# The value projection of three chunks by seven products for eight, and an emission clock that counts PSUM banks

## The chip, the cores and the metric

The kernel runs on one core of a Trainium2 chip. The metric is the time of the program on the device in microseconds (us); the profile adds, for one execution, every instruction's start and duration on each engine: TensorE (PE; its weight loads are listed as PEld), VectorE (DVE), ScalarE (ACT), GpSimd (POOL) and SyncE (SP, which here only issues DMAs).

## What is computed

Two layers, each an attention block A and a feed-forward block B, with the same weights in both. S = 2048 rows, D = 1024, F = 3584, everything in bf16 at the interface.

```python
def _A_ref(x, wqkv, wo):
    H = 32; Dh = D // H
    W, dil = 8, 2
    qkv = (x @ wqkv).reshape(B, S, 3, H, Dh) ...   # q, k, v
    idx = pos[:, None] - off[None, :]              # each row sees 8 rows: itself, -2, ..., -14
    logits = jnp.einsum("bhsd,bhswd->bhsw", q, kg) * scale
    attn = _softmax(jnp.where(mask, logits, -1e9), axis=-1)
    o = jnp.einsum("bhsw,bhswd->bhsd", attn, vg)
    return o... @ wo

def _B_ref(x, w1, w3, w2):
    return (silu(x @ w1) * (x @ w3)) @ w2

x = x + _A_ref(_layernorm(x), A_wqkv, A_wo)
x = x + _B_ref(_layernorm(x), B_w1, B_w3, B_w2)
# and both once more
```

## The kernel before

**Tiling.** The rows are cut in four chunks of 512 (`CH`); a pair (layer, chunk) is a unit, units 0 to 7. The normalised rows of a unit are written transposed (features on the partitions) into `xnT`, of which two buffers exist. q, k and v of a chunk are computed by `q_part`: for each of eight blocks of 128 output features, eight matmuls of 128x512 accumulate in one PSUM bank (L836), ScalarE copies the bank to SBUF (L840), and each pair of blocks is stored to DRAM (`qkv_d`, L847). Attention reads it back in halves of 256 rows: VectorE multiplies and adds in trees (`score_steps` from L576, `value_steps` from L647), TensorE gathers the heads (L604), VectorE takes the maximum and subtracts it (L625, L628), ScalarE takes the Exp (L629), and GpSimd's queue broadcasts the result (L644). The output projection is `o_tile` (L771).

**Order of the units.** q, k and v of all chunks of layer 0 come first, then the B stages of units 0 to 7 (`b_stage`). After the B stages of units 1, 2, 3 and 4 stand q, k and v of units 4, 5, 6 and 7, that is of layer 1's chunks.

**Seven products for eight.** The B stages of units 2 to 7 use Winograd's form of the two-by-two block product (`products`, `pipeline`): the features and the rows are split in halves, and seven products P1 to P7 of half size take the place of eight. For each group of 512 output features one product is eight matmuls of 128x256 (L1052). The block sums of the weights are made once, during units 0 and 1: ScalarE scales a block to FP16 (L910), VectorE forms four sums and differences (`differences`, L922), and GpSimd's queue stores them in DRAM (`t_d`). They come back as an "early" tile of 1 MB (for P1, P5, P6, P2) and a "late" tile of 768 KB (for P7, P3, P4). The sums of `xnT` are made by VectorE in `norm_sums` (L298), in three buffers that all units share; the fourth is made in place in `xnT`, once nothing needs the plain rows. In `pipeline`, a group's P1, P5, P6, P2 alternate with the group before's P7, P3, P4:

```python
for i in range(n + 1):
    for name, tail in (("P1", "P7"), ("P5", "P3"), ("P6", "P4"), ("P2", None)):
```

PSUM banks A, B and D of a group are linked by copies: P1 is copied from A to B (L1064) before P6 may add to A; P5 is kept aside (L1069); A is copied after P6 (L1073) and added to D (L1076) before P3; after P7, VectorE combines A with the kept P5 into the corner (L1088 or L1090), which P4 waits for. In the B stages the last group's tail is filled with the first products of w2 (L1165).

**What sets the order.** No scheduler reorders the instructions: each engine's queue holds them as the Python code emits them. The code carries its own clocks while it emits: `now["pe"]`, `now["dve"]`, `now["act"]` and those of the DMA. `pe`, `dve`, `act` and `dma` advance them by fixed costs. `background(until)` lets VectorE's queued work (sums, normalisations, trees) in where by these clocks it ends before the given time; `act_background` does so for ScalarE up to `gate`, 2.2 us beyond TensorE's clock; `pe_requests` emits a gather of heads once its input is 3.5 us old. `between` lets weight loads, output projections and normalisations in. Weights come through six buffers in the order of the list `seq`; `release(n)` frees buffers and so lets the next n loads go to SP's queue. Six PSUM banks serve the matmuls (`psum`), two the gathers and the output projection (`side`).

Of the kernel before, what the change touches and what calls it, by code (L numbers as in the profile page):

```python
# [17 lines left out]
def kernel(  # L18
# [137 lines left out]
    opened = [0]  # L156

    def side_tile(*args, **kw):

        while opened[0]:  # L160
            assert head(makes) is not None
            take(makes)
        return side.tile(*args, **kw)

    def bank(name):
        if name == "po":
            return side_tile([P, 512], FP32, name=name, tag="sd")
        return psum.tile([P, 512], FP32, name=name, tag="mm")
# [48 lines left out]
    size2 = const.tile([P, 16], FP32, name="size2")  # L217
    total = const.tile([P, 1], FP32, name="total")
# [4 lines left out]
    h16 = hT[:].bitcast(FP16)  # L223
    t2_d = [dram.tile([P, 7, (b - a) // 2, 512], FP16, name=f"t2_d{i}") for i, (a, b) in enumerate(fsplits)]
    t_d = [[dram.tile([P, 14, KT // 2, P], FP16, name=f"t_d{m}_{g}") for g in range(NG)] for m in range(2)]
    qkv_d = [[dram.tile([P, KT, S], BF16, name=f"qkv_d{l}_{i}") for i in range(3)] for l in range(2)]
# [74 lines left out]
    adds, acts, makes, reads, parts, sizes = [], [], [], [], [], []  # L301
# [61 lines left out]
    def act_background():  # L363
        for queue in (acts, sizes, parts, reads):
# [211 lines left out]
    def score_steps():  # L576

        V = nc.vector
        for g, (l, h) in enumerate(halves):
# [20 lines left out]
            def gather_heads(t, parts_=parts_):  # L600
                at["L"] = L = side_tile([P, W, BLK], FP32, name="L", tag="sd")
                for i in range(parts_):
# [24 lines left out]
            def exps():  # L627
                V.tensor_tensor(L[:], L[:], mx[:].unsqueeze(1).to_broadcast([P, W, BLK]), op=ALU.subtract)  # L628
                nc.scalar.activation(E[:], L[:], ACTF.Exp, scale=scale)  # L629
                at["E"] = act(0.65, now["dve"] + 0.1, "exp")  # L630

# [47 lines left out]
    for u in range(len(units)):  # L679
# [14 lines left out]
        if 1 <= u and u + 3 < len(units):  # L694
            seq += [("qkv", which, h) for which in range(3) for h in range(2)]
    w_tiles, w_at, due, used = [], {}, [], [0]

    def load_weight(pieces=1):
# [25 lines left out]
        else:  # L724
# [4 lines left out]
            if rest[0]:  # L729
                got = {}  # L730
                parts.append([weight_size(*rest[0], w, at, got), None])
                reads.append([weight_sums(*rest[0], w, got), None])
# [22 lines left out]
    def o_tile():  # L755
# [12 lines left out]
        for hh in range(2):  # L768
            ps = bank("po")
            for t in range(KT):  # L770
# [6 lines left out]
            dve(0.64, r)  # L777
# [6 lines left out]
    def queue_q(q):  # L784
# [4 lines left out]
        
# [30 lines left out]
    def q_part(l, c, which, ws, then=()):  # L820
# [8 lines left out]
        for t0 in range(0, KT, SG):  # L829
            i = (c * 3 + which) * KT // SG + t0 // SG  # L830
            i = i % (7 if l == 0 else 8) * SG
            sgt = big[:, i * CH:(i + SG) * CH].bitcast(BF16).rearrange("p (a t) -> p a t", a=SG) if l == 0 else hT[:, i:i + SG, :]
            for t in range(t0, t0 + SG):
                ps = bank("ps")
                for kk in range(KT):
# [6 lines left out]
                if first:  # L842
                    nc.scalar.copy(kT[:, t, HALO:], ps[:, 0:TCH])
                    done = act(0.3)
                if t < t0 + SG - 1:
                    pe_requests(2)
            nc.sync.dma_start(qkv_d[l][which][:, t0:t0 + SG, c * CH:(c + 1) * CH], sgt)  # L847
            landed = dma(256, done)
            if l == 0:
                stored[:] = landed, landed  # L850
# [6 lines left out]
        if which == 1:  # L857
            plain_left.discard(("Q", l, c))
        if which == 2:
# [56 lines left out]
    pending, stored, made, held = [0] * 2, [0.0] * 2, set(), []  # L916
    junk = hsum[:].bitcast(BF16).rearrange("p k t -> p (k t)")

    def differences(m, g, a, r):

        b = blocks[a]
# [3 lines left out]
        pending[a] -= 1  # L925
# [487 lines left out]
```

## Time and profile before

| what | value |
|---|---|
| median of 3 runs (lowest, highest) | 1532.38 us (1532.05, 1533.98) |
| the profiled execution | 1532.70 us |
| its span, first to last instruction | 1531.0 us |
| q, k, v of units 4 to 7 (L836), starts at | 514, 701, 885 and 1073 us |
| B stages by seven products, first matmul at | 556 us |
| VectorE's tree products, 128x2048 (L590, L665) | 1.22 us each |
| VectorE's sums of 1024 FP16 elements (L298) | 0.69 us each |
| ScalarE's copy of a bank (L840, L1064) | 0.585, 0.575 us |
| early tile, issue to landing | 6.9 us (median) |

A page of the profile has the busy time of each engine, the span in 40 slices, the DMA queues, the chain of work that ended last (followed back from the last instruction, each step to what released it), the costliest groups of instructions (line, engine, operation, output<-input, shapes, count, busy us, mean ns of one, idle time before them and what ended it) and the DMA issues. Besides the page, single views can be asked for: the chain in order of time (start, duration, what), the waits (who waited for whom, total us, times, longest) and the timeline of a stretch (start, duration, instruction, in brackets the idle time before it and what ended it). Matmuls overlap, so that the mean of one is its latency and not what it adds to the run.

### The profile page before, as it was taken

The page shows a single profiled execution, that of the slowest core. Times are in us where ns is not written, and L with a number is a line of the kernel's source. Part 1 is how long each engine was busy: PE and PEld are TensorE (multiplying, and loading weights), DVE is VectorE, ACT ScalarE, POOL GpSimd, SP SyncE. Part 2 cuts the span into 40 slices and gives each one's busy share as a digit, 9 for nine tenths or more (in the row PEclk, how much of TensorE's full clock was granted, in tenths as well). Part 3 has the DMA queues.
Part 4 walks back from the last instruction along what each step waited for, and adds up shares of the span by engine and source line. Part 5 has one row for each costly group of instructions (what it writes and reads, how often), then busy time and mean ns, then how long its engine had stood idle before and what let it go on. Part 6 is the DMA issues. An engine that isn't in the chain of part 4 may idle for free.

```text
span 1531.0 us, 25095 instructions
## 1 busy us (share of the span) xinstructions
PE 1518.1 (99%) x9594; PEld 989.5 (65%) x9634; DVE 1201.8 (78%) x2126; ACT 884.1 (58%) x1388; POOL 153.7 (10%) x308
## 2 busy tenths in 40 slices
PE   9999999999999999999999999999999999999999
PEld 7666644444444577575786767766677767686865
DVE  4688998889989898989698958898678986435445
ACT  3885476567665357455565564756557445554643
POOL 1210102121211101001011010100111000000000
PEclk9999999999999999999999999999999999999999
DMA  9777969798997888979779997898969988878885
GB/s 321 202 218 215 253 226 330 272 304 289 306 320 247 280 316 294 347 264 303 263 269 324 346 268 282 280 323 302 323 225 333 338 296 282 306 272 334 318 294 203
DMA packets 261432, 439.56 MB, mean 287 GB/s; under 512 B 73856, under 2 KB 201088, under 8 KB 245056
## 3 DMA queue, kind: packets, MB, share of 16 engines
q1 hardware_dynamic: 248464, 390.90, 76.8%
q0 software_dynamic: 12704, 46.93, 8.6%
q8 instruction: 75, 1.23, 0.3%
q14 instruction: 45, 0.37, 0.1%
q10 hardware_dynamic: 144, 0.13, 0.0%
HBM read 345.90 MB, written 67.90 MB: 270 GB/s over the span
## 4 chain that ended last, share of the span: by engine, by line
PE 97%; ACT 1%; issue 1%; DVE 0%; DMA 0%; SPq 0%; ACTq 0%
PE st L1052 32%; PE ps L836 21%; PE w L1165 16%; PE po L771 7%; PE pg L1279 6%; PE pu L1288 6%; PE acc L1310 6%; PE pq L444 1%; PE L L604 0%; DMA wqkv<-in_A_wqkv_dram 0%; ACT L629 0%; ACT L1227 0%; ACT E L629 0%; ACT sg L1227 0%; DVE x_sb L1150 0%
## 5 line engine op out<-in xcount | busy, mean ns | idle before, releaser
L836 PE MATMUL ps<-xnT,wqkv 128*128 128x512 f16 (+1 forms) x1469 | 320.4, 379 | 0.2
L1052 PEld LDWEIGHTS <-early 128*128 128x128 f16 x2688 | 262.6, 98 | 40.4 <-issue 3.5
L836 PEld LDWEIGHTS <-wqkv 128*128 128x128 bf16 x1472 | 210.6, 144 | 108.1 <-issue 2.2
L1165 PE MATMUL w<-t,hT 128*128 128x512 f16 x1008 | 226.0, 379 | 0.6 <-ACT big L1185 0.5
L1052 PEld LDWEIGHTS <-late 128*128 128x128 f16 x2016 | 197.2, 98 | 30.6 <-issue 2.5
L590 DVE TENSOR_TENSOR tree<-qT,kT 128x2048 bf16<-128x2048 bf16 x128 | 156.3, 1221 | 35.8 <-DMA kT<-qkv_d 18.2
L1052 PE MATMUL st<-xnT,late 128*128 128x256 f16 x1344 | 174.2, 273 | 2.2 <-ACT big L1073 2.2
L510 DVE TENSOR_TENSOR tree<-tree 128x1024 bf16<-128x1024 bf16 x256 | 175.6, 686 | 0.9
L1052 PE MATMUL st<-big,early 128*128 128x256 f16 x1344 | 172.3, 273 | 1.6 <-ACT sg L1227 1.1
L1165 PEld LDWEIGHTS <-hT 128*128 128x128 f16 x1008 | 98.2, 98 | 112.9 <-DVE hT L1136 2.0
L1052 PE MATMUL st<-xnT,early 128*128 128x256 f16 x1344 | 165.7, 273 | 0.0
L665 DVE TENSOR_TENSOR tree<-At,vT 128x2048 bf16<-128x2048 bf16 x128 | 156.2, 1221 | 11.9 <-DMA At<-E 10.7
L1064 ACT COPY st<-st 128x512 f32<-128x512 f32 x84 | 48.3, 575 | 128.1 <-PE st L1052 127.4
L771 PE MATMUL po<-wo,oT 128*128 128x512 bf16 x486 | 110.8, 379 | 1.3
L840 ACT CAST hT<-ps 128x512 bf16<-128x512 f32 x96 | 55.8, 585 | 90.6 <-PE ps L836 88.3
L1288 PE MATMUL pu<-xnT,w3t 128*128 128x512 f16 x448 | 105.8, 379 | 0.0
L1279 PE MATMUL pg<-xnT,w1t 128*128 128x512 f16 x448 | 105.8, 379 | 0.0
L1310 PE MATMUL acc<-w2t,hT 128*128 128x512 bf16 x437 | 97.8, 379 | 0.6
L1076 DVE TENSOR_TENSOR st<-st,big 128x512 f32<-128x512 f32 x84 | 58.4, 695 | 46.9 <-ACT big L1073 46.8
L1227 ACT ACTIVATE sg<-st,down_scale 128x512 bf16<-128x512 f32 x126 | 86.6, 687 | 11.6 <-PE st L1052 11.0
L1052 PE MATMUL st<-big,late 128*128 128x256 f16 x672 | 87.1, 273 | 0.0
L771 PEld LDWEIGHTS <-oT 128*128 128x128 bf16 x512 | 50.1, 98 | 55.7
(167 smaller groups left out, 1916.6 us busy)
## 6 DMA issues: line engine op xcount, KB each, us to landing
early<-t_d SPq DMA_DIRECT2D x84, 1024.0 KB, 6.9
late<-t_d SPq DMA_DIRECT2D x84, 768.0 KB, 6.2
t<-t_d SPq DMA_DIRECT2D x42, 1024.0 KB, 7.3
t<-t_d SPq DMA_DIRECT2D x42, 768.0 KB, 5.3
wqkv<-in_A_wqkv_dram SPq DMA_DIRECT2D x28, 1024.0 KB, 8.1
w1t<-in_B_w_dram SPq DMA_DIRECT2D x14, 1024.0 KB, 7.6
w3t<-in_B_w_dram SPq DMA_DIRECT2D x14, 1024.0 KB, 11.0
t_d<-big POOLq DMA_DIRECT2D x28, 512.0 KB, 6.2
```

Of the source, the lines that this page charges most:

```text
L510: nc.vector.tensor_tensor(b, b, buf[:, 4:8, :], op=ALU.add)
L590: V.tensor_tensor(pr, qT[:], kT[:, :, k0:k0 + TCH], op=ALU.mult)
L665: V.tensor_tensor(tm.rearrange("p w (a e) -> p w a e", a=4), At[:].rearrange("p a w e -> p w a e"), win, op=ALU.mult)
L771: nc.tensor.matmul(ps[:], lhsT=oT[:, t, j * P:(j + 1) * P], rhs=wo[:, t, hh * 512:(hh + 1) * 512], start=(t == 0), stop=(t == KT - 1))
L836: nc.tensor.matmul(ps[:], lhsT=ws[kk // KH][:, kk % KH, t::KT], rhs=xnT[:, kk, :], start=(kk == 0), stop=(kk == KT - 1))
L1052: nc.tensor.matmul(out[:, a, :], lhsT=w[:, a, blk, k, :], rhs=rhs[:, k, :], start=start and a == 0 and k == 0, stop=k == KQ - 1, skip_grou ...
L1076: nc.vector.tensor_tensor(G["D"][:], G["D"][:], su, op=ALU.add)
L1165: nc.tensor.matmul(out[:], lhsT=lhs[:, k, j * P:(j + 1) * P], rhs=w[:, k, :], start=start and k == 0, stop=k == nq - 1, skip_group_check=True)
L1227: nc.scalar.activation(sg[:], src, ACTF.Silu, scale=inv)
L1279: nc.tensor.matmul(pg[:], lhsT=w1t[:, kk, fi * P:(fi + 1) * P], rhs=xnT[:, kk, :], start=(kk == 0), stop=(kk == KT - 1))
L1288: nc.tensor.matmul(pu[:], lhsT=w3t[:, kk, fi * P:(fi + 1) * P], rhs=xnT[:, kk, :], start=(kk == 0), stop=(kk == KT - 1))
L1310: nc.tensor.matmul(acc[:], lhsT=hT[:, f, j * P:(j + 1) * P], rhs=tiles[hh][f // nq][:, f % nq, :], start=(f == 0), stop=(f == f1 - f0 - 1))
```

## The change

v of units 5, 6 and 7 (layer 1's chunks 1 to 3) is computed by seven products: two groups of 512 output features, in `pipeline`, by the new function `v_products`. The block sums of v's weights are made once, in unit 4's stage after the B stage of unit 1. There v is now computed first, then q, then k, and v's two weight buffers are held until the sums are made. The scale of the weights needs the sum of their squares, which ScalarE takes in eight passes of 1024 elements in a new queue of lowest priority (`lazy`) while layer 0's q, k and v are computed. In the stages of units 5 to 7, q and k stay plain, and the sums of `xnT` are also made for v.

The second part is in the clocks: `turn` and `free` keep, for each of the two PSUM pools, the time at which each bank's last reader is done, and a new tile pushes `now["pe"]` to the time of the bank that it takes. Every place that takes a bank records it. `finish_sums` lets other VectorE work in before the step that it forces, and w2's scalings are put ahead of queued weight scalings that nothing waits for yet.

The diff, cut to its core (the recording of banks is shown once for each kind):

```diff
+    rings = dict(mm=[], sd=[])
+    def turn(tag, bufs):
+        ring = rings[tag]
+        if len(ring) >= bufs:
+            now["pe"] = max(now["pe"], ring[-bufs])
+        ring.append(0.0)
+        return ring, len(ring) - 1
+    def free(at, t):
+        ring, i = at
+        ring[i] = t + 0.1
+    def mm_tile(shape, name):
+        turns["mm"] = turn("mm", 6)
+        return psum.tile(shape, FP32, name=name, tag="mm")
...
+    size_v = const.tile([P, 8], FP32, name="size_v")
+    blocks += [hT[:, 9:16, :].bitcast(FP16).rearrange("p b (k c) -> p b k c", k=KT // 2)]
+    t_d += [[dram.tile([P, 14, KT // 2, P], FP16, name=f"t_dv_{g}") for g in range(2)]]
...
-        for queue in (acts, sizes, parts, reads):
+        for queue in (acts, sizes, parts, reads, lazy):
...
-            seq += [("qkv", which, h) for which in range(3) for h in range(2)]
+            seq += [("qkv", which, h) for which in ((2, 0, 1) if u == 1 else (0, 1)) for h in range(2)]
+            if u > 1:
+                seq += [("early", 2, 0), ("early", 2, 1), ("late", 2, 0), ("late", 2, 1)]
...
             ps = bank("po")
+            slot = turns["sd"]
...
-            dve(0.64, r)
+            free(slot, dve(0.64, r))
...
+        if q > NCH:
+            adds.append([sum_later(key), None])
...
+    def size_of_v(i, w, at):
+        for k in range(KH):
+            yield 1.10, at, lambda: nc.scalar.activation(junk[:, 0:D], w[:, k], ACTF.Square,
+                                                         accum_out=size_v[:, KH * i + k:KH * i + k + 1])
+        if i == 1:
+            total_scale(size_v, up_v, down_v, got_v)
+    def sums_of_v(ws, at):
+        while "at" not in got_v:
+            yield "blocked"
+        stored[2] = at
+        for g in range(2):
+            for a in range(2):
+                while pending[1] and pending[2]:
+                    yield "blocked"
+                slot = min((i for i in (1, 2) if not pending[i]), key=lambda i: stored[i])
+                pending[slot] += 1
+                b = blocks[slot]
+                for i, (kh, fh) in ((0, (0, 0)), (1, (0, 1)), (3, (1, 0)), (5, (1, 1))):
+                    t = 4 * g + 2 * fh + a
+                    yield 0.65, max(at, got_v["at"], stored[slot]), lambda: nc.scalar.activation(
+                        b[:, i], ws[kh][:, :, t::KT], ACTF.Copy, scale=up_v[:])
+                makes.append([differences(2, g, a, now["act"] + 0.1, slot), None])
+        made.add("v")
...
+    def v_products(l, c):
+        key = ("Q", l, c)
...
+        def consume(G, q, src, r):
+            pair, t0 = q % 2, HT * (q // 2)
+            to = stage(G, pair)
+            if q != 3:
+                nc.scalar.activation(to[:, :, t0:t0 + HT], src, ACTF.Copy, scale=down_v[:])
+                r = act(0.57, r)
+            end = r
+            G["left", pair] -= 1
+            G["at", pair] = max(r, G.get(("at", pair), 0.0))
+            if not G["left", pair]:
+                t = 4 * G["g"] + 2 * pair
+                nc.sync.dma_start(qkv_d[l][2][:, t:t + SG, c * CH:(c + 1) * CH], to)
...
+        pipeline(key, groups, consume, lambda i: between(False, i == 0), True)
+        xnT_free[key] = now["pe"]
...
+            if (c, which) == (1, 0):
+                for i in range(2):
+                    lazy.append([size_of_v(i, w_tiles[4 + i], 40.0), None])
...
-            for which in range(3):
-                if which == 2:
-                    between(False, True)
-                q_part(*units[q], which, [weight("qkv"), weight("qkv")])
+            if u == 1:
+                for which in (2, 0, 1):
+                    if which == 1:
+                        between(False, True)
+                    ws = [weight("qkv"), weight("qkv")]
+                    if which == 2:
+                        ready = max(w_at[used[0] - 1], now["pe"])
+                        reads.append([sums_of_v(ws, ready), None])
+                    q_part(*units[q], which, ws, (), 1, 4)
+                    if which == 2:
+                        continue
+                    if which == 0:
+                        finish_sums(lambda: "v" in made)
+                        release(2)
+                    release(2)
+                force(makes, lambda: not any(pending))
+                continue
+            for which in range(2):
+                q_part(*units[q], which, [weight("qkv"), weight("qkv")], (), 1)
                 release(2)
+            v_products(*units[q])
```

In the changed file the lines move: the matmuls of `pipeline` stand at L1118 there, its copies at L1132 (P1), L1138 (P5) and L1142 (P6), the Exp at L656 and the plain projections at L869.

## The prediction

> **What bounds the kernel now.** I read the page's busy table and chain first, to see which engine sets the end; then the groups by line, for what one matmul costs; then the list of waits on TensorE, for what is left besides matmuls; then the timeline around the longest of these waits.
>
> ```profile
> span 1531.0 us, 25095 instructions
> ...
> PE 1518.1 (99%) x9594; PEld 989.5 (65%) x9634; DVE 1201.8 (78%) x2126; ACT 884.1 (58%) x1388; POOL 153.7 (10%) x308
> ...
> PE 97%; ACT 1%; issue 1%; DVE 0%; DMA 0%; SPq 0%; ACTq 0%
> ```
>
> TensorE is the bound: 97% of the chain is PE. A busy PE need not be at its peak, so I take the cost of a matmul from the chain in order of time, where uninterrupted runs stand:
>
> ```profile
> 830.14 34.93 PE st L1052 x320
> ...
> 895.83 31.23 PE ps L836 x144
> ```
>
> A product of 256 columns ("st", the seven-product form) costs 34.93/320 = 0.1092 us, one of 512 columns ("ps", plain q, k, v) 31.23/144 = 0.2169 us there, with a small gap inside; the neighbouring run of 48 gives 10.36/48 = 0.2158, which I use. The means of 379 and 273 ns in the groups are latencies of overlapping matmuls and are not added up.
>
> ```profile
> PE st L1052 <- ACT big L1073: 2.2, 1, 2.2
> ...
> PE st L1052 <- ACT sg L1227: 1.1, 1, 1.1
> PE w L1165 <- ACT big L1185: 0.5, 1, 0.5
> PE st L1052 <- ACT st L1064: 0.4, 1, 0.4
> ```
>
> What is left besides matmuls in layer 1: single waits for ScalarE. From the starts of successive matmuls they are 1.25 us (at 668), 2.36 (987), 0.63 (1065), 0.28 (1159) and 0.57 (1233), together 5.1 us; the view shows less because ends are modelled. Layer 0 has no wait above 0.22 us after 10 us. The longest one, in the timeline:
>
> ```profile
> 983.33 0.69 DVE L628 TENSOR_TENSOR L<-L,mx 128x512 f32<-128x512 f32 x1
> ...
> 984.19 1.28 ACT L629 ACT_TABLE_LOAD   x1
> 985.48 0.60 ACT L629 ACTIVATE E<-L 128x512 bf16<-128x512 f32 x1
> 986.10 1.28 ACT L1227 ACT_TABLE_LOAD   x1
> ...
> 989.16 0.58 ACT L1073 COPY big<-st 128x512 f32<-128x512 f32 x1
> ...
> 989.79 1.03 PE L1052 MATMUL st<-xnT,late 128*128 128x256 f16 x8 [2.19 <-ACT big L1073]
> ```
>
> The softmax's Exp stands in ScalarE's queue ahead of four copies that TensorE needs. Between the start of its table load and the end of the copy at L1073 lie 5.55 us. All five waits are of this kind: they depend on where the emission puts one Exp.
>
> [...]
>
> **The change, part by part.** (Starts and orders are from the instruction order of the changed kernel; durations from the trace of before.)
>
> *Matmuls.* Three chunks lose 64 products of 512 columns each, 192 x 0.2158 = 41.4 us, and gain 2 groups x 7 x 8 of 256 columns each, 336 x 0.1092 = 36.7 us. All lie on TensorE, which is the path: **-4.7 us**. The one size matmul in layer 0 costs about 0.1 (0.11 us behind each such matmul in the trace).
>
> *Work on the other engines, beside the matmuls.* ScalarE loses 24 copies (0.585) and gains 8 squares of 1024 (about 1.1, as L318), 16 scalings (0.71, as L910) and 36 evacuations (about 0.62): +27 us of 647 idle. VectorE gains 16 differences (0.42), 12 sums (0.69) and 12 combinations (0.7): +23 us of 329 idle. The squares are in layer 0, where each copy has six banks (6 x 1.73 us) of room. The scalings need 11 us of ScalarE in v and q of u=1, which last 28 us and hold 9 us of copies. I take zero for both; if that cover is gone, a late block delays only loads needed 14 us later. Two loads of 1 MB give way per chunk to four, 3.5 MB in all; they are issued before or in the k part, 14 to 28 us ahead, against 7 us to landing: zero, up to 2 us in all. The stores of t_dv go past POOL's queue ahead of At, which waits for VectorE there anyway (310.8 us in the waits): zero. On SP the v stores wait for ScalarE as before.
>
> *The end of each v pass.* Unlike the feed-forward's, its last P3 is followed by P4 with no w2 product between. P4 needs the corner that VectorE makes from P7: 0.2 us to start, 0.75 (L1088), 0.05 to release, against 0.87 of P3 as cover: 0.13 us at least. VectorE is in order, and ahead of the corner stand queued trees. Counting from the k part's end (it releases the in-place P7 sum, which heads the queue), with operations that overlap a little (0.62 for 1024 elements, 1.15 for 2048), the first chunk's corner ends at 11.9 to 12.5 us, P3 at 11.4: 0.85. In the second no tree stands there: 0.15. In the third 0.5. Sum **+1.5 us**; bounds 0.4 and 4.
>
> *The start of each v pass.* P6 waits for the copy of P1 (0.2 + 0.57 + 0.05), covered by P5 (0.87). In the third chunk two normalisations (L345, 1.24 each) stand among the last copies, so that copy ends at 2.7 us after the k part, where P6 could start at 1.75: **+1.0**. In the second an Exp stands there, counted below. Bounds 0 and 3.
>
> *The Exps.* Order and clock change throughout. I worked each of the last nine of them through from the gather's matmul. Four fall in q parts or w2 steps or a place with slack: 0. The second of layer 1 (behind P3 in a group): 0.4. The one before the second v pass: table load 1.75 to 3.0 us after the gather, Exp to 3.65, two copies, then P1's copy to 5.45 against 5.2: 0.3. One repeats the pattern above: load from 2.9, 5.55 to the copy, so 8.45 against TensorE's 6.1: 2.4. The last, between w2's P6 steps: 0.7. The rest are 0 to 0.1. Together 3.9 where there were 5.1: **-1.2**; bounds -5 (none waits) and +5 (each costs what the worst did in two more places).
>
> *Sum.* -4.7 + 0.1 + 1.5 + 1.0 - 1.2 = -3.3 us. The profiled execution took 1532.70 (span 1531.0 and 1.7 around it); the median is 1532.38, 0.3 lower, and the difference is applied to it: **1529.0 us**. A measurement of this kernel can tell about 0.2%, 3.1 us, so this is just beyond it.
>
> **Rivals.** (B) *The clock also clears the Exps.* Now that the emission pushes TensorE's clock when a bank is not free, copies and Exps may be placed without collision. For: all five waits are misplacements of one instruction. Against: the repeated pattern that I find in the order. It gives -4.7 + 0.1 + 2.5 - 3.8 = -5.9: 1526.5.
> (C) *The short passes give it back.* Each of the three pays some 1.2 us at its start and 1.4 at its end, as its two groups don't overlap with anything: -4.7 + 0.1 + 7.8 - 1.2 = +2.0 at worst, about 0 with half of the Exp waits gone as well; I take 1532.0. For: VectorE is at 8 to 9 tenths in these slices. Against: a queue of only one or two trees before each corner.
> (D) *VectorE becomes the bound from 556 to 1242 us*, and the kernel is slower. There it is busy 579.6 of 685.5 us by the windows (85%), and in B stages 0.90. The passes add 5.5 us each to a queue that holds the trees of attention; between a product and its dependent lie about four passes, 3.5 us. From the point where its backlog exceeds that, each added microsecond appears on TensorE and the output projection waits for its trees too. With half of the 16.6 added us on the path beside the sum above: -3.3 + 8.3 = +5.0: 1537.4. Against: it idled 7.59 us in the k part of the last chunk for a transpose, so there is slack.
>
> **How the numbers follow.** Forecast 0.52 (its own range 1527.6 to 1530.4), B 0.16, C 0.19, D 0.13. Faster by over 0.2% (below 1529.3): B and six tenths of the forecast's, 0.49. Slower (above 1535.4): D, 0.13. Within: the rest, 0.38. The range goes from 1526.8, which leaves out half of B, to 1533.6, which leaves out nearly all of D.
>
> **What would show it.** The "st" count rises from 4704 to 5040 and plain "ps" falls by 192; the run of st stays at 0.109 us each, else the first term falls. The three v passes last 12.2 us and 0.1 to 1.9 more; waits of P4 for the corner and of P6 for P1's copy appear there. One wait of about 2.4 us for L1142's copy stands before a w2 step near the end of attention. VectorE busy rises by about 23 us, ScalarE by 27. The forecast is wrong if new waits stand in layer 0, if TensorE waits for a weight's landing, or if the waits for ScalarE in B stages differ from 3.9 by over 2 us.

## The result, and the profile after

| | before | after |
|---|---|---|
| median (lowest to highest) | 1533.18 us, 4 runs (1532.05 to 1534.65) | 1554.88 us, 4 runs (1553.24 to 1559.4) |
| the profiled execution, its span | 1532.70, 1531.0 us | 1554.44, 1552.6 us |

The ratio is 1.0146, with a 95% interval of 1.0122 to 1.0169. The changed kernel is 22 us slower, where 3 us of gain had been forecast.

The page of the changed kernel, the same lines as were shown of before (span, busy time, chain by engine):

```profile
span 1552.6 us, 25595 instructions
...
PE 1523.5 (98%) x9780; PEld 996.0 (64%) x9780; DVE 1222.2 (79%) x2171; ACT 917.4 (59%) x1432; POOL 162.6 (10%) x316
...
PE 53%; DVE 10%; DMA 3%; ACT 3%; issue 2%; POOL 0%; DVEq 0%; ACTq 0%; POOLq 0%
```

The busy times changed about as worked out (VectorE +20 us for +23, ScalarE +33 for +27), and by them nothing is wrong. The third line tells where to look: PE was 97% of the chain and is 53%. It has to be read with care, since this chain can be followed back only to 435.8 us, so that it covers 72% of the span. In the part that it covers PE is 74%; the rest runs through VectorE, ScalarE and transfers. A run of half-width products on this chain still has its length of before:

```profile
1223.24 34.93 PE st L1118 x320
```

so the products themselves didn't slow down. What TensorE waits for (the list of waits, in us in all, times, longest; the first nine):

```profile
PE pu L1405 <- DMA w3t<-in_B_w_dram: 3.1, 1, 3.1
PE st L1118 <- ACT big L1142: 2.9, 3, 2.2
PE ps L869 <- ACT big L873: 2.6, 1, 2.6
PE acc L1429 <- DMA w2t<-in_B_w_dram: 2.4, 2, 1.5
PE st L1118 <- ACT hT L873: 2.2, 1, 2.2
PE po L802 <- DVE oT L540: 1.7, 2, 1.5
PE w L1273 <- ACT big L1296: 1.7, 4, 0.5
PE st L1118 <- DVE hT L1157: 1.4, 2, 1.1
PE pg L1394 <- DMA w1t<-in_B_w_dram: 1.3, 1, 1.3
```

Four of these lines are in layer 0, where there was no wait above 0.22 us: three landings of feed-forward weights (6.8 us) and a copy of a bank (2.6). Only the eighth belongs to the v passes. To place the loss, I take from the traces when the first product of some stages starts (one execution each; the stages before are all in the number):

| kernel | first product of unit 2's B stage | q of unit 5 | B stage of unit 6 | span |
|---|---|---|---|---|
| before | 556.3 | 700.7 | 1257.5 | 1531.0 |
| after | 573.6 | 720.7 | 1279.0 | 1552.6 |
| squares_unseen | 555.5 | 699.9 | 1258.4 | 1531.9 |
| squares_empty | 571.3 | 715.9 | 1279.3 | 1552.7 |
| v_unseen | 559.6 | 709.7 | 1264.1 | 1538.0 |
| sums_only | 558.0 | 709.5 | 1268.5 | 1542.0 |
| ring6 | 556.0 | 706.0 | 1260.2 | 1534.0 |
| priced | 556.2 | 703.9 | 1257.4 | 1530.9 |
| after_repriced | 555.2 | 707.3 | 1266.7 | 1540.3 |

Of after's 21.6 us of span, 17.3 are lost before the first half-width product, 2.7 in the B stage of unit 2, and 1.4 between unit 5's q and unit 6's B stage, where the three passes stand; after that nothing. TensorE's own time closes this account. From the starts of successive matmuls, its waits above 0.3 us sum to 26.8 us in after (16.3 of them before the first half-width product) and to 4.8 us in before. Three stretches of 3.41 us at half clock, read in the last section, cost another 1.7 us each. With 4.7 us less of products this makes 22.4 us, for 21.6 measured.

### The profile page after: what moved, and what is told of

It is laid out like the page before. It is cut to its first block, busy times and chain, and to the rows that moved or that the text cites. A ratio compares the mean times of both kernels' runs of the same rounds, so it can differ in the third digit from the quotient of the medians.

```text
span 1552.6 us, 25595 instructions
## 1 busy us (share of the span) xinstructions
PE 1523.5 (98%) x9780; PEld 996.0 (64%) x9780; DVE 1222.2 (79%) x2171; ACT 917.4 (59%) x1432; POOL 162.6 (10%) x316
## 3 DMA queue, kind: packets, MB, share of 16 engines
q8 instruction: 76, 1.25, 0.3%
## 4 chain that ended last, share of the span: by engine, by line
PE 53%; DVE 10%; DMA 3%; ACT 3%; issue 2%; POOL 0%; DVEq 0%; ACTq 0%; POOLq 0%
PE st L1118 29%; PE w L1273 14%; PE ps L869 6%; PE po L802 5%; DMA t_d<-big 2%; DVE tree L616 1%; DVE tree L693 1%; DVE tree L536 1%; DMA w3t<-in_B_w_dram 1%; DVE hT L1349 1%; DVE big L958 1%; DVE hT L1243 1%; DVE big L324 1%; ACT sg L1338 0%; ACT big L1075 0%
## 5 line engine op out<-in xcount | busy, mean ns | idle before, releaser
L1118 PEld LDWEIGHTS <-early 128*128 128x128 f16 x2880 | 282.3, 98 | 44.0 <-DMA early<-t_d 2.7
L869 PE MATMUL ps<-xnT,wqkv 128*128 128x512 f16 (+1 forms) x1280 | 279.8, 379 | 2.6 <-ACT big L873 2.6
L869 PEld LDWEIGHTS <-wqkv 128*128 128x128 bf16 x1280 | 182.9, 144 | 97.0 <-issue 5.4
L1118 PEld LDWEIGHTS <-late 128*128 128x128 f16 x2160 | 211.2, 98 | 38.3 <-issue 8.6
L1118 PE MATMUL st<-xnT,late 128*128 128x256 f16 x1440 | 186.6, 273 | 4.7 <-ACT big L1142 2.9
L1118 PE MATMUL st<-big,early 128*128 128x256 f16 x1440 | 186.1, 274 | 0.9 <-ACT st L1132 0.7
L1118 PE MATMUL st<-xnT,early 128*128 128x256 f16 x1440 | 177.6, 273 | 2.2 <-ACT hT L873 2.2
L616 DVE TENSOR_TENSOR tree<-qT,kT 128x2048 bf16<-128x2048 bf16 x128 | 156.3, 1221 | 22.5 <-DMA qT<-qkv_d 16.8
L1132 ACT COPY st<-st 128x512 f32<-128x512 f32 x90 | 51.9, 576 | 124.3 <-PE st L1118 123.0
L802 PE MATMUL po<-wo,oT 128*128 128x512 bf16 x512 | 116.2, 379 | 2.4 <-DVE oT L540 1.7
L1118 PE MATMUL st<-big,late 128*128 128x256 f16 x720 | 93.4, 273 | 1.1 <-DVE st L1145 1.1
L1338 ACT ACTIVATE sg<-st,down_scale 128x512 bf16<-128x512 f32 x126 | 86.7, 688 | 11.5 <-PE st L1118 11.2
L1405 PEld LDWEIGHTS <-w3t 128*128 128x128 bf16 x448 | 44.0, 98 | 56.9 <-DMA w3t<-in_B_w_dram 3.6
## 6 DMA issues: line engine op xcount, KB each, us to landing
w3t<-in_B_w_dram SPq DMA_DIRECT2D x14, 1024.0 KB, 12.4
```

The source lines that it names most:

```text
L616: V.tensor_tensor(pr, qT[:], kT[:, :, k0:k0 + TCH], op=ALU.mult)
L802: nc.tensor.matmul(ps[:], lhsT=oT[:, t, j * P:(j + 1) * P], rhs=wo[:, t, hh * 512:(hh + 1) * 512], start=(t == 0), stop=(t == KT - 1))
L869: nc.tensor.matmul(ps[:], lhsT=ws[kk // KH][:, kk % KH, t::KT], rhs=xnT[:, kk, :], start=(kk == 0), stop=(kk == KT - 1))
L1118: nc.tensor.matmul(out[:, a, :], lhsT=w[:, a, blk, k, :], rhs=rhs[:, k, :], start=start and a == 0 and k == 0, stop=k == KQ - 1, skip_grou ...
L1338: nc.scalar.activation(sg[:], src, ACTF.Silu, scale=inv)
L1405: nc.tensor.matmul(pu[:], lhsT=w3t[:, kk, fi * P:(fi + 1) * P], rhs=xnT[:, kk, :], start=(kk == 0), stop=(kk == KT - 1))
```

## The experiments

My first theory was that the eight squares cost the loss: they stand in layer 0's emission and so change what the emission puts where in everything after it. In one form it is their price in the emission's clocks, in another ScalarE's own time for them. The rivals were the bank clock and v's sums in unit 4's stage. Each batch of kernels ran beside the kernel before, whose median was 1532.2 to 1533.4 us from batch to batch; so a difference between kernels of two batches is uncertain by about 1 us. In the quoted texts, which were written batch by batch, "theory 3" means the bank clock up to v_contiguous and the short ring of staging slots from ring6 on.

### One part alone, and the whole without the clock

*clock_only*: before, with the bank clock (`turn`, `free`) and nothing else of the change.

```diff
+        if len(ring) >= bufs:
+            now["pe"] = max(now["pe"], ring[-bufs])
```

> The kernel before with the bank-counting emission clock alone: v of every chunk plain, no squares, no sums of v. Theory 1 (the loss begins with the squares of v's weights, which move everything after them in layer 0): within 0.2% of before, 1531 to 1535 us. Theory 2 (the sums of v in unit 4's stage and the short passes cost it): the same. Theory 3 (the new clock puts work in the wrong places): 1545 us or more.

Measured: 1536.88 us, ratio 1.0024 [1.0015, 1.0034]. The clock alone costs 4 us, a little more than theories 1 and 2 allowed and far less than theory 3 asked.

*squares_only*: before, with the eight squares and the scale, under the old clock; nothing uses them. w2's scalings stand ahead of others in the queue, as in the changed kernel.

```diff
+            if (c, which) == (1, 0):
+                for i in range(2):
+                    lazy.append([size_of_v(i, w_tiles[4 + i], 40.0), None])
...
-                        reads.extend([sums_of_w2(split, f, tiles, max(times[0] + times[1])), None] for f in steps)
+                        i = next((i for i, item in enumerate(reads) if item[2] not in held), len(reads))
+                        reads[i:i] = [[sums_of_w2(split, f, tiles, max(times[0] + times[1])), None, None] for f in steps]
```

> The kernel before with the eight squares of v's weights and the scale made from them, which nothing uses; old clock, v plain. Theory 1: 8 to 16 us slower than before (1541 to 1549), with waits for w1, w3 or w2 tiles in the B stages of units 0 and 1. Theories 2 and 3: within 3 us of before, since 8 x 1.1 us of ScalarE lie in idle time.

Measured: 1558.01 us, ratio 1.016 [1.0143, 1.0177]. Eight instructions of 1.06 us cost 26 us, in the direction of theory 1 but more than the 8 to 16 us that it gave.

*v_only*: the whole change with `turn` pushing no clock, the old `finish_sums`, and w2's scalings queued at the end as before.

```diff
-        if len(ring) >= bufs:
-            now["pe"] = max(now["pe"], ring[-bufs])
...
-                        i = next((i for i, item in enumerate(reads) if item[2] not in held), len(reads))
-                        reads[i:i] = [[sums_of_w2(split, f, tiles, max(times[0] + times[1])), None, None] for f in steps]
+                        reads.extend([sums_of_w2(split, f, tiles, max(times[0] + times[1])), None, None] for f in steps)
```

> The whole change but with the old emission clock and the old order in finish_sums. Theory 1: 1545 to 1553 us, near the changed kernel, as the squares are in it. Theory 2: the same. Theory 3: about 1530 us, the matmuls' 4.7 us less waits of 1 to 2 us.

Measured: 1676.26 us, ratio 1.0928 [1.0903, 1.0953]. No theory expected that. With the squares in the order, the three parts that v_only undoes (the clock, the new `finish_sums`, the place of w2's scalings) together save some 120 us; which of them does is not shown. In its trace 12 of w2's scalings still stand in unit 4's stage, which lasts 139.1 us for 42.1 in before.

*v_no_squares*: the changed kernel without the squares, under the old clock and with the old `finish_sums`. It differs from v_only in two things, the squares and the place of w2's scalings, which are ahead again as in the changed kernel.

```diff
-        for k in range(KH):
-            yield 1.10, at, lambda: nc.scalar.activation(junk[:, 0:D], w[:, k], ACTF.Square, ...
+        if i == 0:
+            nc.gpsimd.memset(size_v[:], 2.5)
+        yield 0.0, at, lambda: None
```

> As v_only, but the eight squares are left out: size_v is filled with a constant, so that the scale of v's weights isn't measured. Theory 1: 1530 to 1536 us, layer 0 as before. Theory 2: 1543 us or more, since the sums of v and the passes are all there. Theory 3: about 1530 us.

Measured: 1541.0 us, ratio 1.005 [1.0035, 1.0065]. 135 us of v_only's loss hang on the squares and on the place of w2's scalings together, and this pair does not part the two: in v_no_squares none of w2's scalings is left for unit 4's stage. 0.5%, some 8 us, remain without either, between what theories 1 and 2 gave.

### Is it the squares' time, or their price in the clocks?

*squares_unseen*: squares_only, but the squares count nothing in the clocks and are issued at set points, and the scale is left out. In the traces, TensorE's and GpSimd's instructions come in the order of before, so that moving w2's scalings ahead changes nothing there by itself.

```diff
-            yield 1.10, at, lambda: nc.scalar.activation(junk[:, 0:D], w[:, k], ACTF.Square,
+            while now["pe"] < 40.0 + 6.0 * (KH * i + k):
+                yield "blocked"
+            yield 0.0, 0.0, lambda: nc.scalar.activation(junk[:, 0:D], w[:, k], ACTF.Square,
...
-        if i == 1:
-            total_scale(size_v, up_v, down_v, got_v)
```

> The kernel before with the eight squares in ScalarE's queue, but at no cost in the emission's clocks and without the scale, so that every other instruction keeps its place. Theory 1a (the squares hurt by what their cost in the clocks makes the emission do to the order): within 3 us of before. Theory 1b (they hurt by the 10 us of ScalarE that they take): most of the 26 us that squares_only lost.

*squares_empty*: squares_only, with each square reading 2 columns for 1024: almost no work, and the order that the full price makes.

```diff
-            yield 1.10, at, lambda: nc.scalar.activation(junk[:, 0:D], w[:, k], ACTF.Square,
+            yield 1.10, at, lambda: nc.scalar.activation(junk[:, 0:2], w[:, k, 0:2], ACTF.Square,
```

> As squares_only, the order of instructions the same, but each square reads two columns instead of 1024 (the sum of squares is so left out), about 0.2 us instead of 1.06. Theory 1a: near squares_only, 1550 us or more. Theory 1b: near before, 1532 to 1536 us.

Measured: 1533.55 us, ratio 1.0005 [0.9996, 1.0014], and 1554.51 us, ratio 1.0143 [1.0128, 1.0158]. The work without the order costs nothing that can be told; the order without the work costs 21.6 of squares_only's 26 us. Both are as the first form expected. The scale, which squares_unseen leaves out, is not the cause either: v_unseen below has it, and there q, k and v of unit 4 start at 514.3 us, for 514.2 in before. So it is the price in the clocks and the order that it makes. The waits of ScalarE and VectorE in layer 0 (from 190 us to 515 and 522) of squares_unseen first, then of squares_empty, show by what way:

```profile
ACT big L938 <- DMA t_d<-big: 7.3, 5, 5.6
...
DVE big L952 <- ACT big L938: 4.6, 7, 1.5
```

```profile
ACT big L938 <- DMA t_d<-big: 30.5, 8, 10.6
...
ACT hsum L906 <- DMA w3t<-in_B_w_dram: 10.2, 2, 7.2
ACT hsum L906 <- DMA w1t<-in_B_w_dram: 5.2, 2, 3.0
...
DVE big L952 <- ACT big L938: 17.3, 9, 5.2
DVE big L1073 <- ACT big L1067: 10.9, 5, 3.7
```

L938 scales a block of the feed-forward weights and L952 makes its sums. A scaling may begin only when the slot's last sums have been stored in DRAM. In the new order it is put where that store is still under way. The longest such wait in squares_empty's timeline, ScalarE and then VectorE (start, duration, what, and in brackets the idle time before it):

```profile
451.29 2.56 ACT L1067 ACTIVATE big<-w2t,up 128x512 f16<-128x512 bf16 x4 [0.65 <-DMA t_d<-big]
464.48 2.56 ACT L938 ACTIVATE big<-w3t,up_scale 128x512 f16<-128x512 bf16 x4 [10.62 <-DMA t_d<-big]
```

```profile
460.64 1.22 DVE L614 TENSOR_TENSOR tree<-qT,kT 128x2048 bf16<-128x2048 bf16 x1
467.06 1.68 DVE L952 TENSOR_TENSOR big<-big 128x512 f16<-128x512 f16 x4 [5.21 <-ACT big L938]
468.66 0.42 DVE L538 TENSOR_TENSOR psm<-tree 128x512 bf16<-128x512 bf16 x1
```

ScalarE stands 10.6 us before the scaling. VectorE stands 5.2 us behind it, with a tree half done whose last step (L538) starts only at 468.7; the same step of the tree before, at 459.1, came right behind the L614 that stands ahead of it. Neither engine ran anything in these gaps of 10.6 and 5.2 us, though later instructions stood behind. The weight buffers whose sums come late are freed late, and the next loads land late; those are the weight waits of TensorE in the list of after. The longest of them can be followed there: SyncE's queue waited 8.1 us for w2's scalings (L1075, the longest wait 4.5) between 426 and 470 us, issued the load of w3 at 457.6, and it landed at 471.4, where TensorE's wait of 3.1 us ends.

*no_squares*: the changed kernel, bank clock included, with the edit of v_no_squares.

> The changed kernel, new clock and all, with the squares alone left out (size_v filled with a constant, so the scale of v's weights isn't measured). If the squares and their order are what the change loses, this is 1530 to 1538 us: about the 1555 of the changed kernel less the 19 us that its stages lose up to 574 us. If the new clock matters as much without the squares as with them, it is well below v_no_squares (1541).

Measured: 1544.32 us, ratio 1.0079 [1.0062, 1.0095]. In the changed kernel itself the squares cost 10.6 us of 22. The time is above the 1530 to 1538 that was expected if they were all of it.

*v_unseen*: the whole change under the old clock and with the old `finish_sums`, the squares as in squares_unseen, the scale with them.

> The whole change with the old emission clock, but with the eight squares unseen by the emission's clocks: they are issued at set points of layer 0 and add nothing to them. Nothing is left out. If it is the squares' price in the emission's clocks that costs layer 0 (theory 1), layer 0 has stalls like the kernel before (under 1 us in every stage), and the time is that of the kernel without squares, 1541 us (1539 to 1543). If ScalarE's time for the squares itself cost something (rival), it is 1545 or more.

Measured: 1539.96 us, ratio 1.0054 [1.0037, 1.007], as expected. Of what costs time, only v's sums and the passes are left of the change.

### What v's sums cost in unit 4's stage

*sums_only*: v_unseen with v of units 5 to 7 by plain products.

```diff
-            for which in range(2):
-                q_part(*units[q], which, [weight("qkv"), weight("qkv")], (), 1)
+            for which in range(3):
+                q_part(*units[q], which, [weight("qkv"), weight("qkv")])
...
-            v_products(*units[q])
```

> As v_unseen, but v of units 5 to 7 by the plain products of before: v's sums are made in the stage of unit 4 and stored, and not used. It tells the cost of the sums and of the order v, q, k from the net of the three passes. If the passes give back about what their products save (4.7 us of products against about 5 us of waits), the time is 1540 to 1543; if the passes gain 3 us as in my sum, 1544; if they lose, below 1539.

Measured: 1543.66 us, ratio 1.0074 [1.0059, 1.0089]. This is near the 1544 of the second case. The sums, made and not used, cost 11 us, and the passes take back 3.7. Part of the latter is the clock: in the profiled executions 10.24 us of sums_only and 3.41 us of v_unseen were at half clock, which, less the idle time in them, is about 4.5 and 1.6 us lost.

*v_contiguous*: v_no_squares with another read in the scaling of v's weights.

```diff
-                        b[:, i], ws[kh][:, :, t::KT], ACTF.Copy, scale=up_v[:])
+                        b[:, i], ws[kh][:, :, t * P:(t + 1) * P], ACTF.Copy, scale=up_v[:])
```

> As v_no_squares, but the scalings of v's weights read 128 neighbouring columns instead of every eighth one, so that v's output columns are in the wrong places. The order of instructions is the same. If the 1.25 us that a strided scaling takes (0.71 for w1's) delays unit 4's stage and what follows, 4 to 8 us faster than v_no_squares: 1533 to 1537. If the order there or VectorE is the cause, 1540 to 1542.

Measured: 1536.41 us, ratio 1.0021 [1.0011, 1.0032]: 4.6 us less than v_no_squares, as expected. The profiled execution was 6 us above this median, so its stalls are not read. The groups of v_unseen show the two prices (busy us, mean ns of one): v's scaling reads every eighth column, w1's and w3's read neighbours.

```profile
L942 ACT ACTIVATE big<-w1t,up_scale 128x512 f16<-128x512 bf16 x56 | 36.1, 711 | 7.6 <-DMA t_d<-big 7.2 <-DVE up_scale L902 0.4
...
L989 ACT ACTIVATE big<-wqkv,up_v 128x512 f16<-128x512 bf16 x8 | 9.6, 1256 | 2.1 <-DMA t_dv<-big 2.1
```

Output and input have the same size and types in the two rows. With the step of eight columns a scaling took 1.256 us, with neighbours 0.711.

*v_qkv_order*: v_unseen with q, k, v in the old order, v's weights loaded first.

```diff
-                for which in (2, 0, 1):
+                held_v = [weight("qkv"), weight("qkv")]
+                reads.append([sums_of_v(held_v, max(w_at[used[0] - 1], now["pe"])), None])
+                for which in range(3):
```

> As v_unseen, but the stage of unit 4 computes q, k, v in that order as before; v's weights are loaded first and their sums are made during q and k. Theory 2 (v ahead of q and k delays k, and with it the first scores of unit 4, by 14 us; VectorE idles there and is behind in the next feed-forward stage): the stalls of the stage of unit 4 and of the one after it fall from about 2.5 + 8 us to under 3 us together, time 1532 to 1536. Rival (the sums' own work on ScalarE and VectorE in that stage costs it, in any order): the stalls stay, time 1539 to 1543.

*qkv_contiguous*: both edits together.

> As v_qkv_order, but each scaling of v's weights reads 128 neighbouring columns in place of every eighth one, so that v's columns of units 5 to 7 stand in other places than the reference's. If the strided read costs what it did in the other order (4.6 us), it is 4 to 5 us faster than v_qkv_order: 1528 to 1531, the first kernel of the change that is not slower than the one before. If with q and k ahead of it there is room enough for the slow scalings, within 1 us of v_qkv_order.

Measured: 1553.48 us, ratio 1.0137 [1.0122, 1.0152], and 1546.53 us, ratio 1.0092 [1.0077, 1.0107]. Both expectations missed. The edit made a wait of its own, at a place where four loads are asked for at once and not two (waits of TensorE in v_qkv_order, 500 to 700 us):

```profile
PE ps L867 <- DMA wqkv<-in_A_wqkv_dram: 10.7, 2, 9.9
PE st L1116 <- DVE st L1143: 4.0, 1, 4.0
```

In the first of these waits TensorE's clock also fell to half, at 516.5 us, and stayed there until 530.2, some 6 us beyond the wait. That makes the pair a poor test of the time. But the second line is the same wait for VectorE that v_unseen has (3.9 us), so a late k is not needed for it, and the theory of k's delay is dropped as the cause of this wait. What stands there instead is in v_unseen's timeline of unit 4's stage. ScalarE:

```profile
531.45 2.43 ACT L989 ACTIVATE big<-wqkv,up_v 128x512 f16<-128x512 bf16 x2 [2.11 <-DMA t_dv<-big]
537.75 0.59 ACT L871 CAST hT<-ps 128x512 bf16<-128x512 f32 x1 [3.87 <-DMA qkv_d<-hT]
538.23 2.38 ACT L989 ACTIVATE big<-wqkv,up_v 128x512 f16<-128x512 bf16 x2
```

and VectorE, with the correction that TensorE waits for at its end:

```profile
534.37 0.42 DVE L538 TENSOR_TENSOR psm<-tree 128x512 bf16<-128x512 bf16 x1
540.64 1.68 DVE L956 TENSOR_TENSOR big<-big 128x512 f16<-128x512 f16 x4 [5.85 <-ACT big L989]
542.25 0.68 DVE L650 TENSOR_REDUCE mx<-L 128x64 f32<-128x512 f32 x1
546.61 1.68 DVE L956 TENSOR_TENSOR hT<-hT 128x512 f16<-128x512 f16 x4 [3.68 <-ACT hT L989]
...
570.02 0.70 DVE L1143 TENSOR_TENSOR st<-st,big 128x512 f32<-128x512 f32 x1
```

The change keeps a block of sums in the upper part of `hT`, so the copies of this stage go round four staging slots (`ring=4`) where they went round eight. A copy at 537.75 waited 3.9 us for the store of its slot (in this stage these stores land 11.0 us after their issue, median); two scalings stood behind it; VectorE stood 5.85 us for these. From 549.6 to 570 VectorE then works without a wait on what it had not done, and L1143, which P3 of unit 2's B stage needs, comes last.

*ring6*: v_unseen with two more slots, in `hsum`, which is idle there. *ring6_contiguous*: the same with the read of v_contiguous.

```diff
+            if ring == 6 and i >= 4 * SG:
+                sgt = spare[:, (i - 4 * SG):(i - 4 * SG) + SG, :]
...
-                    q_part(*units[q], which, ws, (), 1, 4)
+                    q_part(*units[q], which, ws, (), 1, 6)
```

> As v_unseen, but the copies of the stage of unit 4 go through six staging slots in place of four (the two new ones in a buffer that is idle there). Theory 3 (the short ring: copies wait for stores, the scalings behind them on ScalarE come late, VectorE waits for these in order and brings its trees and corners late): ScalarE's waits for the stores of staging slots (4.8 us) are gone, the stalls of this stage and the next fall from 2.2 + 6.7 us to under 5 together, time 1535 to 1537. Rival (the slow scalings alone make ScalarE late): the stalls stay, 1539 to 1541.

> As ring6, with the scalings reading 128 neighbouring columns, so that v's columns of units 5 to 7 stand in other places than the reference's. If ring and strided read together make the whole cost of the sums, both stalls are nearly gone and the time is 1529 to 1533, no slower than the kernel before. If the 6.5 us stall after the stage stays, as it did with neighbouring columns and four slots (1536.4), a third cause is there.

Measured: 1536.42 us, ratio 1.0022 [1.0015, 1.003], and 1531.14 us, ratio 0.9996 [0.9986, 1.0006]. Two slots save 3.5 us with strided reads and 5.3 with neighbouring ones; neighbouring reads save 4.6 us with four slots and 5.3 with six. Of these four differences only the last is between kernels of one batch. The two causes add up to 8.8 of the 11 us. In ring6 ScalarE's waits for the stores of staging slots are gone and unit 4's stage has its length of before (42.1 us); but the B stage after it is still 150.0 us long, for 144.4 before. VectorE still waits up to 3.7 us for the slow scalings, and TensorE 3.7 us for L1147, the correction there. From the end of this wait on TensorE ran at half clock until 571.4 us, which is some 2.7 of the 5.6 us. In ring6_contiguous its clock did not fall.

*priced*: v_unseen, with the emission told nearly what a scaling costs. *ring6_priced*: this and the ring. *priced_100*: 1.00 in place of 1.15.

```diff
-                    yield 0.65, max(at, got_v["at"], stored[slot]), lambda: nc.scalar.activation(
+                    yield 1.15, max(at, got_v["at"], stored[slot]), lambda: nc.scalar.activation(
```

> As v_unseen, but the emission counts 1.15 us for a scaling of v's weights in place of 0.65 (the strided read takes 1.25). Theory 4 (the emission puts the differences too early in VectorE's queue, as it thinks the scalings done): VectorE's waits for scalings (9.8 us in that stage) fall under 3 us, time 1534 to 1537. If ScalarE's waits for staging slots set the lateness (theory 3), most of them stay: 1538 to 1541.

> ring6 and priced together. If each takes away a part, this is the fastest of the four with nothing left out, 1532 to 1535; if both act on the same wait, as ring6.

> As priced, with 1.00 us for a scaling in place of 1.15: another order of the work, still nearer the measured 1.25 than 0.65 is. If the price's distance from the truth counts, it lies between v_unseen (1540.0) and priced (1533.5), nearer the latter: 1533 to 1537. If priced was one lucky order, it may be anywhere, 1538 or more as well.

Measured: 1533.48 us, ratio 1.0006 [0.9998, 1.0015]; 1533.23 us, ratio 1.0008 [1.0001, 1.0015]; 1542.26 us, ratio 1.0065 [1.0047, 1.0083]. In all three VectorE's waits for v's scalings are gone from the list of that stage, as the theory has it. priced is 0.5 us faster than expected, ring6_priced no faster than priced within the noise, and priced_100 missed the 1533 to 1537 that a truer price would give: the time does not follow. With 1.00 another instruction stands behind the copy that waits for its slot, an Exp, and VectorE waits for that (waits of VectorE in priced_100, 508 to 580 us):

```profile
DVE sm__5089 L660 <- ACT E L654: 5.7, 1, 5.7
```

In priced that wait is 4.6 us. priced_100 loses its 9 us to other waits, among them 4.0 us of TensorE's for late tiles in unit 2's B stage and one of 3.3 us at the start of the first v pass. So priced is partly a favourable order, not a proof that a truer price is a faster one.

*after_repriced*: the changed kernel, bank clock included, with the squares of squares_unseen and the price of priced.

> The changed kernel as it is, bank clock included, with two corrections of the emission's prices alone: the squares count nothing in the clocks and a scaling of v counts 1.15 us for 0.65. Nothing is left out. If the two prices make the loss and the bank clock adds what it did alone (about 4 us) to priced's 1533.5, it is 1535 to 1538; if the clock's cost was itself one of collisions with the mis-priced operations, 1532 to 1534; if the prices are not what costs the changed kernel, over 1544.

Measured: 1542.52 us, ratio 1.0061 [1.0044, 1.0078]. That lies between the expected ranges. The two prices bring back 12.4 us of 22, and the loss ahead of the first half-width product is gone (556.3 us before, 555.2 here). The other 9 us are in the stages after it: there TensorE's waits above 0.3 us are 19 and sum to 18.1 us, where the old clock's order of priced has 8 with 9.1 us. Whether the bank clock or the new `finish_sums` makes this order, no run parts. Of the kernels that leave nothing out none was faster than the one before; priced equals it.

## Why the prediction was wrong

The step that failed is in "Work on the other engines, beside the matmuls": "The squares are in layer 0, where each copy has six banks (6 x 1.73 us) of room. The scalings need 11 us of ScalarE in v and q of u=1, which last 28 us and hold 9 us of copies. I take zero for both". For the time of the squares zero was right (squares_unseen, 1.0005). For their order and for the scalings it was not: 10.6 us and 11 us. What it left out is that the order is written by a program with clocks: 1.1 us in a clock moves what is emitted after it, and the new order put scalings where the stores that free their slots were still under way. The working followed the new order around the passes and not in layer 0.

By its terms:
- *Matmuls, -4.7.* Right: 5040 "st" and 1280 "ps", the run of 320 still 34.93 us.
- *Start and end of the v passes, +2.5.* In after, from the starts of the products, 0.35 and 0.72 us at the starts and 1.25, 0.13 and 0.47 at the ends: 2.9. sums_only against v_unseen gives -3.7 for the passes in all, the clock's part included; -3.3 was predicted for the whole change.
- *Exps, -1.2.* The wait of 2.4 us for L1142's copy is there, 2.36 from 1192.2 on. But from 583 us on, waits above 0.3 outside the v passes sum to 6.5, not 3.9; not all of these are Exps.
- *Squares, 0.* 10.6 us in the changed kernel, through the order.
- *Scalings, 0.* "0.71, as L910" was the wrong row, because L910 reads neighbouring columns; it is 1.25, 20 us for 11. And "hold 9 us of copies" took no account of the ring that shrinks from eight slots to four. Sums and order of the stage: 11 us. "a late block delays only loads needed 14 us later" missed VectorE's queue behind the block.
- *The bank clock* had no term of its own. Alone it costs 4 us; with the new `finish_sums`, no_squares against v_unseen gives 4.4 and against v_no_squares 3.3.
- Two sums are slightly off and change nothing: ScalarE's terms make +28 us and not +27, and the chance of "faster" is 0.47 and not 0.49.

11.2 for the sums, -3.7 for the passes, 4.4 for the clock and 10.6 for the squares make 22.5, for 21.7 measured. This is no test of the parts: they are the steps of one chain of kernels (before, sums_only, v_unseen, no_squares, after) and must add up. In another order the parts differ: in before the squares cost 26 us, in the changed kernel 10.6. The sum over TensorE's waits and clock in the section on the result does not hang on such a chain.

Rival D came nearest in kind, since VectorE's lateness reaches TensorE, but not by the work added: its busy time rose by 20 us and it idled longer (24.7 us for 14.4 in the B stage of unit 1, 16.4 for 6.8 in unit 4's stage). The last paragraph had named the signs: new waits in layer 0 and waits for a weight's landing.

Open: why v_only is so very slow (TensorE waits 44 us for VectorE's oT in it, up to 15.3 at once), and whether the squares would cost as much there with w2's scalings ahead; what the new `finish_sums` does on its own; by which single placement the squares' price turns layer 0's order bad; and where the last 2.4 us of the sums' 11.2 lie, which ring and read don't explain, and how much of the 11.2 is the clock's.

## What to carry to other kernels

Where the program writes the order by its own cost model, an instruction that is free on its engine can still cost through the order it causes: run it once unpriced and once priced but empty, and the two are told apart. Before calling added work on an idle engine free, list what each instruction waits for (a slot's store, a staging ring made smaller) and what stands behind it in order on the next engine. Take a duration from a row with the same access pattern, not only the same shape (here 1.256 us for 0.711). When a kernel is taken apart by runs, let two of them differ in one thing; v_only and v_no_squares differ in two, and their difference can't be read.

## What was not expected of the hardware

TensorE's clock fell to half three times in the changed kernel, each time within 1.0 us after the end of an idle gap: gaps of 3.31, 2.40 and 2.36 us, from 468.2, 571.2 and 1192.2 us on, were followed by 3.41 us at half clock, from 472.0, 574.4 and 1195.6 us on. In these stretches products of 512 columns start 0.427 us apart, for 0.216 otherwise, and products of 256 columns 0.213, for 0.109. Two of them, in busy time by stretch (PE, PEld, DVE, ACT, POOL; the last three numbers are granted clock, DMA share, GB/s):

```profile
470.10:475.60 5.50, 4.12 (x12) 1.56 (x13) 5.37 (x8) 4.51 (x7) 2.18 (x4) 0.69 1.07 387
...
1193.50:1198.50 5.00, 3.90 (x16) 1.93 (x16) 4.92 (x8) 3.34 (x5) 2.27 (x4) 0.71 1.26 219
```

A mean of 0.69 over 5.5 us is 3.4 us at half clock, and costs about 1.7 us beside the gap. The length of a gap alone doesn't tell whether the clock falls. A gap of 2.78 us in the changed kernel, from 136.0 us on, had no stretch at half clock behind it, nor had the gaps of 2.36 us in the kernel before, from 987.4 on, and in priced, from 1172.4 on. The same gap in squares_unseen, from 986.7 on, was followed by 3.41 us at half clock.

The clock records show a regularity. In the changed kernel the second stretch, the third and a last one at the program's end start 102.40, 723.63 and 1082.03 us after the first: 30, 212 and 317 times 3.413 us, the length of a stretch. I cut the two traces into steps of this length, counted from the first stretch in the changed kernel and from the one at the program's end (1530.84) in the kernel before. Of the three gaps with a fall behind them, two lie within one step, and the third has 2.93 of its 3.31 us in one. Two gaps without a fall are parted: the one at 136.0 at 137.5, into 1.45 and 1.34 us, and the one at 987.4 in the kernel before at 988.1, into 0.69 and 1.67 us. That it matters where a gap falls in these steps is my estimate from these five gaps; no run of this case tests it.

The cost shows in the times too: of the 50 executions of before beside ring6, the 25 with a mean clock of 1.000 have a median of 1531.85 us, the 25 with 0.999 one of 1533.60.
